# Expert units in one phase per batch behind the middle attention stage, both expert counts in one visit, three query buffers

## The chip, the cores and the metric

The kernel runs on one core of one Trainium2 chip. The metric is the device time of an execution in microseconds, the median of three: 462.71 us (462.43 to 462.92). Engines are called as in the profile: PE is TensorE (PEld its weight loads), DVE VectorE, ACT ScalarE, POOL GpSimd, SP the engine that issues most DMAs. Lines such as L251 are lines of the kernel before.

## The reference

Multi-query attention feeds a mixture of experts. Attention has 8 batches, 16 query heads of 384 positions by 64 features, and one key and value head per batch:

```
scores = (q @ k.T) / 8;  attn = softmax(scores);  o = attn @ v
x = o, rearranged to 3072 tokens x 1024 features
```

Each token goes to one of 4 groups and one of the group's 4 experts (16 in all), by two argmaxes:

```
g_idx = argmax(x @ w_group);  e_idx = argmax(x @ w_expert[g_idx])
y = relu(x @ w1[g_idx, e_idx]) @ w2[g_idx, e_idx]
out = softmax weight of the group * softmax weight of the expert * y
```

The weights w1 and w2 are 1024 x 1024 per expert. Inputs are float32.

## The kernel before, in words

**Stages.** The sequence of a batch is cut into three tiles of 128 query positions. One tile is a *stage* p, 0 to 23; p = 3b + st, b the batch, st the tile. A stage computes on PE scores of tile p (`scores`, L251: six key blocks j of 64 keys, 8 matmul records each), and the value products of tile p-1 (`values`, L290, also six blocks). ACT takes the exponential of each score block into a tile `pt` (L253). DVE adds the six blocks of a tile up (`pre_add`, L259 and L261), folds the sum over keys (`fold_keys`, L265), and PE sums the folded tile over partitions (`join`, L273: it reads `fold`). DVE inverts and spreads the sums (`invert`, L278 and L280) and multiplies the values by them (`weigh`, L300), which gives x of the tile, transposed; POOL casts it to bf16. The value products accumulate in a single buffer `o`, so values of tile p start only when tile p-1 is weighed. The join of tile p-1 stands in the middle of stage p, after its third value block.

**Turning the queries.** The queries come in with positions on partitions in blocks; DVE turns them (`prep_q`, L243) into a tile `qT` with two buffers, `prep_k` (L233) turns the keys.

**Experts.** Attention over nearly equal weights makes the tokens of a batch alike, so almost all of them go to one expert: for each batch one expert is chosen on the chip, its weights are loaded, and all 384 tokens of the batch go through it, with a gate of zero where a token belongs elsewhere. The work for a batch is a list of fourteen *units*: eight first-layer units (`h_unit`, L407: 8 matmuls of 384 columns, ACT applies relu, L408) and six second-layer units (`y_unit`, L415: 8 matmuls of 512 columns, ACT scales by the selected gate `gsel`, L416, and the row tile `y` is stored). `fill(n)` (L451 on) runs the next n units of whatever batch is next.

**Choice and counts.** `gates(b)` runs the gate matmuls (L312) on PE and the argmax and softmax arithmetic on DVE: for the first tile of batch b (`choose_a`) and for the other two of batch b-1 (`gate_math`; its one-hot is L373). `counts(now, full)` (L333 on) counts expert use by a matmul with ones: for the first tile of batch `now` (L338), from which `choose_b` picks the expert and POOL issues its weight loads (L145, L357), and for all of batch `full` (L340), from which `gate_c` marks pairs of batch and expert still missing and makes `gsel`. ACT copies the counts out of PSUM (L342).

**The leftover pair.** One pair of batch and expert that isn't covered is known early (`early_pair`, L508 on); its weights are loaded by `leftover_w1` and `leftover_w2` when a fixed number of units has run, and its few tokens are gathered, computed and scattered at the end. If more were missing, a slow path behind a branch would take over. `bound_a` and `bound_b` (L478 on) test a bound on the scores for which a softmax without its maximum is safe.

**What sets the order.** The order of instructions on every engine is the order in which this program calls the functions; each engine works through its own in that order, with semaphores between them. `PHASES` (L497) says how many units follow a stage: a *phase* stands between the end of a stage and the next stage's scores. In a phase, `steps` names what is called after which unit. Batch 0's first three units stand inside stage 4. After stage 23 the last join, values and weigh follow, and the last twenty units are spread among the work on the leftover pair.

Of the kernel before, what the change touches and what calls it, by code (L numbers as in the profile page):

```python
# [9 lines left out]
FP32 = mybir.dt.float32  # L10
# [3 lines left out]
P = 128  # L14
# [7 lines left out]
def kernel(  # L22
# [96 lines left out]
    def load_first():  # L119
        kt = pool.tile([P, ST, 2, D], FP32, tag="k", bufs=2, name="kn")  # L120
        qt = pool.tile([P, ST, HP, 2, D], FP32, tag="qraw", bufs=2, name="qn")
        for a in range(2):
            nc.scalar.dma_start(out=kt[:, :, a], in_=kn)
        for c in range(2):
            hs = slice(c * HC, (c + 1) * HC)
            for a in range(2):
                (nc.scalar if c and a else nc.sync).dma_start(out=qt[:, 0, hs, a], in_=qn[0, :, a, hs])
        for a in range(2):
            nc.sync.dma_start(out=qt[:, 1, :, a], in_=qn[1, :, a])
        k_raw[0], q_raw[0] = kt, qt  # L130
        load_k(1)
        load_v(0)
        for a in range(2):
            nc.sync.dma_start(out=qt[:, 2, :, a], in_=qn[2, :, a])
        qe_in = q[1].rearrange("(a hp) (st p) d -> st p a hp d", a=2, p=P)
        qe = pool.tile([P, HP, 2, D], FP32, tag="y", bufs=4, name="qe")
        for a in range(2):
            nc.sync.dma_start(out=qe[:, :, a], in_=qe_in[0, :, a])
        q_nat.append(qe)
# [80 lines left out]
        nc.vector.tensor_copy(out=kT[0][:], in_=ps[:, 0:S])  # L220

    def turn_q(p, nat, copies):
        qT[p] = pool.tile([P, 2 * CW], FP32, tag="qT", bufs=2, name="qT")
        n = HP // len(copies)
        for i, copy in enumerate(copies):
            ps = side([P, 2 * CW], FP32, "qps")
            for h in range(n):
                nc.tensor.transpose(out=ps[:, h * P:(h + 1) * P], in_=nat(i * n + h).rearrange("p a d -> p (a d)"), identity=ident[:])
            copy(out=qT[p][:, i * n * P:(i + 1) * n * P], in_=ps[:, 0:n * P])  # L229
# [9 lines left out]
        return q_raw[b][:, :, st * (P // 32):(st + 1) * (P // 32)].rearrange("p h k d -> p h (k d)")  # L239

    def prep_q(p):
        qT[p] = pool.tile([P, 2 * CW], FP32, tag="qT", bufs=2, name="qT")
        nc.vector.transpose(out=qT[p][:].rearrange("p (h n) -> p h n", h=HP), in_=q_of(p))  # L243

    def scores(p, j):
# [87 lines left out]
    def counts(now, full):  # L333
        n = GE * (1 + ST)
        ps = side([P, n], FP32, "cps")
        lo, hi = (0 if now is not None else GE), (n if full is not None else GE)
        if now is not None:
            nc.tensor.matmul(out=ps[:, 0:GE], lhsT=ones_bf[:], rhs=first[now][:].rearrange("p g e -> p (g e)"), start=True, stop=True)  # L338
        if full is not None:
            nc.tensor.matmul(out=ps[:, GE:n], lhsT=ones_bf[:], rhs=ohe_t[full][:].rearrange("p s g e -> p (s g e)"), start=True, stop=True)  # L340
        t = pool.tile([P, n], FP32, tag="cnt1", bufs=2, name="cnt1")
        nc.scalar.copy(out=t[:, lo:hi], in_=ps[:, lo:hi])  # L342
        if now is not None:
            seen[now] = t[:, 0:GE]
            choose_b(now, t[:, 0:GE])
        if full is not None:
            gate_c(full, t[:, GE:n])
# [78 lines left out]
    def first_units(b):  # L426
        rows = {}

        def place(st, cs):
            if cs.start == 0:  # L430
                rows[st] = pool.tile([P, Dm], FP32, tag="y", bufs=4, name="y")
            return rows[st][:, cs]

        def store(st, cs, y):
            if cs.stop == Dm:
                nc.sync.dma_start(out=outv[b, :, st, :], in_=rows[st][:])
        return moe_units(wts[b][0], wts[b][1], xbf[b], lambda: gsel[b], place, store)
# [13 lines left out]
    def fill(n):  # L451
        while n > 0:
            if not units:
                if begun[0] >= B or begun[0] not in wts:
                    return
                units.extend(first_units(begun[0]))
                begun[0] += 1
            units.pop(0)()
            n -= 1
            ran[0] += 1  # L460
            if ran[0] == (FO + 2 * ST) * (B - 2) + FO:
                leftover_w1()
            if ran[0] == (FO + 2 * ST) * (B - 1):
                leftover_w2()

    def gates(b):
        if b == 0:
            choose_a(0, gate_a(0, 0, 1))
            return
        ps = gate_a(b, 0, ST)  # L470
        choose_a(b, ps)
        gate_logits(b - 1, ps, 1, ST)
        gate_math(b - 1)
# [4 lines left out]
    def bound_a():  # L478
        sq = pool.tile([P, 2], FP32, tag="sq", bufs=1, name="sq")
        nc.vector.reduce_max(out=sq[:, 0:1], in_=stat_q[:], axis=AX)  # L480
        nc.vector.reduce_max(out=sq[:, 1:2], in_=stat_k[:], axis=AX)
        bound["sq"] = sq
# [11 lines left out]
        nc.vector.tensor_copy(out=oki[:], in_=okf[:])  # L494
        bound["okf"] = okf

    PHASES = {4: 5, 6: 7, 7: 6, 9: 7, 10: 6, 12: 7, 13: 6, 15: 7, 16: 6, 18: 7, 19: 6, 21: 7, 22: 7, 23: 5}  # L497

    def gates_and_turns(p):
        b = p // ST  # L500
        gates(b)
        if b + 1 < B:
            prep_k(b + 1)
            prep_q(p + 2)

    leftover = {}

# [38 lines left out]
    for p in range(NP):  # L546
        b, st = divmod(p, ST)
        jobs = [lambda: gates(0), lambda: None, lambda: counts(0, None)] if p == 2 else []
        if p == 0 or p == ST or (st == 1 and 1 < b < B - 1):
            load_q(b + 1)  # L550
        for j in range(3):
            scores(p, j)
            if p == 0 and j == 0:
                turn_q(1, lambda h: q_raw[0][:, 1, h], [nc.vector.tensor_copy])
        if p == 0:
            stats_k(0)
            prep_k(1)
        elif p == ST:
            prep_q(p + 1)
        if jobs:  # L560
            jobs.pop(0)()
        for j in (1, 2):
            pre_add(p, j)
        for j in range(KB):
            if p > 0:
                values(p - 1, j)
            if j == 2 and p > 0:
                join(p - 1)
            if j + 3 < KB:
                scores(p, j + 3)  # L570
            if 0 < j < 4:
                pre_add(p, j + 2)
            if j == 2 and p > 0:
                invert(p - 1)
            if j == 3:
                stats_q(p)
                if p == 1:
                    turn_q(2, lambda h: q_raw[0][:, 2, h], [nc.scalar.copy])
                elif p == 2:
                    turn_q(3, lambda h: q_nat[0][:, h], [nc.scalar.copy])  # L580
            if jobs:
                jobs.pop(0)()
            if p == ST + 1 and j == 0:
                fill(3)
            if st == 1 and 0 < b < B - 1 and j == 0:
                load_k(b + 1)
            if 0 < j < 5:
                some_q(1 if p <= ST + 1 else 2)
            if st == 1 and b + 1 < B and j == KB - 1:
                load_v(b + 1)  # L590
        assert not jobs
        if p > 0:
            weigh(p - 1)
        fold_keys(p)
        if st == 2 and b + 1 < B:
            stats_k(b + 1)
        if p in PHASES:
            n = PHASES[p]
            steps = {}
            if st < 2:  # L600
                prep_q(p + 1)
            if st == 0:
                counts(None, b - 2)
            elif st == 1:
                steps = {2: lambda: gates_and_turns(p), n - 1: lambda: counts(b, None)}
            else:
                bound_a()
                steps = {0: lambda: (counts(None, b - 1), early_pair()), n - 1: bound_b}
            for i in range(n):
                fill(1)  # L610
                if i in steps:
                    steps[i]()
# [6 lines left out]
    fill(2)  # L619
    gate_logits(last, gate_a(last, 1, ST), 1, ST)  # L620
    gate_math(last)
    fill(2)
    counts(None, last)

    xe = pool.tile([P, KO, S], BF16, tag="qraw", bufs=2, name="xe")
    nc.sync.dma_start(out=xe[:].rearrange("p k s -> p (k s)"), in_=xb_dram[bass.ds(leftover["b"], 1)].rearrange("a p k -> (a p) k"))
# [63 lines left out]
    for ko in range(KO):  # L690
        for st in range(ST):
            nc.tensor.matmul(out=px[:, ko, :], lhsT=xtok[st][:, ko * P:(ko + 1) * P], rhs=pick_bf[:, st, :], start=(st == 0), stop=(st == ST - 1))
    xc = pool.tile([P, KO, CAP], BF16, tag="qT", bufs=2, name="xc")
    nc.vector.tensor_copy(out=xc[:], in_=px[:])

    w1c, w2c = leftover["w1"], leftover["w2"]
# [6 lines left out]
    phT = side([P, 2, P], BF16, "phT")  # L703
    for h in range(2):
        nc.tensor.transpose(out=phT[:, h, :], in_=hg[:, h * P:(h + 1) * P], identity=ident_bf[:])
    hc = pool.tile([P, 2, P], BF16, tag="qT", bufs=2, name="hc")
    nc.vector.tensor_copy(out=hc[:], in_=phT[:])
    py = side([P, QW], FP32, "py")
    for g in range(4):
# [153 lines left out]
```

## Time and profile before

| what | value |
|---|---|
| time | 462.71 us (462.43 to 462.92) |
| span of the profiled execution | 462.0 us, granted PE clock 0.994 |
| PE busy | 450.8 us |
| DVE busy | 305.7 us |
| ACT busy | 242.6 us |
| POOL busy | 60.4 us |
| score matmuls (L251) and value matmuls (L290) | 142.8 and 141.0 us |
| unit matmuls, first layer (L407) and second (L415) | 87.4 and 85.4 us |
| loads of expert weights from issue to landing | 10.1 us (quarter of w1), 21.6 us (w2) |

Engines work side by side, so their busy times don't add up to the span. Matmuls are pipelined and their ends are modelled: the durations printed for neighbouring matmuls overlap, and the distance between the starts of two pieces is the better measure of what a piece costs.

### The profile page before, as it was taken

How to read it: one execution, taken by the hardware profiler on the slowest of the kernel's cores; microseconds unless marked ns; L12 is line 12 of the kernel's file. 1: busy time of each engine (PE TensorE's matmuls, PEld its weight loads, DVE VectorE, ACT ScalarE, POOL GpSimd, SP SyncE). 2: the span in 40 equal slices, each digit the busy share in tenths (PEclk: the TensorE clock that was granted, in tenths of full speed). 3: DMA queues.
4: the chain of work that ended last, by engine and by line, in shares of the span. 5: the costliest groups of instructions: out<-in, count | busy, mean ns of one | idle time of the engine just before them, and what ended most of it. 6: DMA issues, size and time to landing. Idle time of an engine off the chain costs nothing. (4 is left out here: it accounts for less than half of the span.)

```text
span 462.0 us, 10131 instructions
## 1 busy us (share of the span) xinstructions
PE 450.8 (98%) x4191; PEld 199.3 (43%) x4191; DVE 305.7 (66%) x483; ACT 242.6 (53%) x351; POOL 60.4 (13%) x83
## 2 busy tenths in 40 slices
PE   8999999999999999999999999999999999999992
PEld 6333444333533445343533435343443535344641
DVE  3999967964879286973779475992779564764400
ACT  2967645636366454745366364745457363623331
POOL 1004003000031002100030001300030000330000
PEclk9999999999999999999999999999999999999997
DMA  7697996998479691996759684996749712799981
GB/s 150 94 153 106 216 215 103 198 252 181 78 116 210 212 191 29 195 226 157 153 88 210 182 163 101 174 234 140 163 90 207 171 47 91 121 212 260 286 218 61
DMA packets 152165, 74.56 MB, mean 161 GB/s; under 512 B 120216, under 2 KB 138652, under 8 KB 152112
## 3 DMA queue, kind: packets, MB, share of 16 engines
q0 software_dynamic: 28416, 37.84, 47.2%
q1 hardware_dynamic: 122368, 35.68, 32.5%
q8 instruction: 35, 0.57, 0.5%
q10 hardware_dynamic: 1328, 0.33, 0.4%
q14 instruction: 18, 0.15, 0.1%
HBM read 92.62 MB, written 19.01 MB: 242 GB/s over the span
## 5 line engine op out<-in xcount | busy, mean ns | idle before, releaser
L253 ACT ACTIVATE pt<-s 128x1024 f32<-128x1024 f32 x144 | 142.1, 1026 | 67.2 <-PE s L251 66.4
L251 PE MATMUL s<-qT,kT 64*64 64x512 f32 x1152 | 142.8, 595 | 0.2 <-ACT qT L229 0.2
L290 PE MATMUL o<-pt,v 64*64 64x512 f32 x1152 | 141.0, 590 | 0.0
L261 DVE TENSOR_TENSOR presum<-presum,pt 128x1024 f32<-128x1024 f32 x96 | 116.6, 1215 | 16.3 <-ACT pt L253 10.9
L407 PE MATMUL hps<-xbf,w 128*128 128x384 bf16 x512 | 87.4, 326 | 0.0
L415 PE MATMUL yps<-w,hT 128*128 128x512 bf16 x384 | 85.4, 379 | 0.6 <-ACT y L416 0.6
L290 PEld LDWEIGHTS o<-pt,v 64*64 64x64 f32 x1152 | 43.5, 133 | 76.9 <-issue 73.2
L259 DVE TENSOR_TENSOR presum<-pt 128x1024 f32<-128x1024 f32 x24 | 29.4, 1224 | 69.3 <-ACT pt L253 68.5
L251 PEld LDWEIGHTS s<-qT,kT 64*64 64x64 f32 x1152 | 40.2, 133 | 64.3 <-issue 52.2
L416 ACT ACTIVATE y<-yps,gsel 128x512 f32<-128x512 f32 x48 | 32.6, 686 | 61.9 <-PE yps L415 49.9
L407 PEld LDWEIGHTS <-w 128*128 128x128 bf16 x512 | 48.6, 98 | 35.7 <-issue 4.1
L301 POOL CAST xbf<-xT 128x1024 bf16<-128x1024 f32 x24 | 25.0, 1041 | 280.8 <-DVE xT L300 280.8
L408 ACT ACTIVATE hT<-hps 128x384 bf16<-128x384 f32 x64 | 31.3, 488 | 51.0 <-PE hps L407 44.0
L415 PEld LDWEIGHTS <-hT 128*128 128x128 bf16 x384 | 36.8, 98 | 47.7 <-issue 4.9
L145 POOL DMA_DIRECT2D w<-in_moe_w_dram x36 | 24.8, 708 | 77.8 <-issue 58.7
L300 DVE TENSOR_TENSOR xT<-o,rinv 128x1024 f32<-128x1024 f32 x24 | 29.2, 1215 | 3.7 <-PE o L290 3.7
L280 DVE STREAM_TRANSPOSE rinv<-rc 128x1024 f32<-128x1024 f32 x24 | 29.9, 1245 | 0.8
L265 DVE TRANSPOSE_TENSOR_REDUCE fold<-presum 128x32 f32<-128x1024 f32 x24 | 29.6, 1232 | 0.0
L243 DVE STREAM_TRANSPOSE qT<-qraw 128x1024 f32<-128x1024 f32 x20 | 24.1, 1202 | 0.0
L209 ACT ACTIVATE qraw<-qraw 128x1024 f32<-128x1024 f32 x21 | 22.0, 1049 | 0.0
L318 DVE STREAM_TRANSPOSE L<-gps 128x32 f32<-128x32 f32 (+1 forms) x16 | 3.6, 227 | 17.4 <-PE gps L312 17.4
L273 PEld LDWEIGHTS sm<-fold,sel 64*64 64x64 f32 x192 | 7.2, 133 | 12.9 <-issue 12.9
(143 smaller groups left out, 158.2 us busy)
## 6 DMA issues: line engine op xcount, KB each, us to landing
w<-in_moe_w_dram POOLq DMA_DIRECT2D x36, 512.0 KB, 10.1
w<-in_moe_w_dram POOLq DMA_DIRECT2D x9, 2048.0 KB, 21.6
out_dram<-y SPq DMA_DIRECT2D x24, 512.0 KB, 2.8
qraw<-in_q_dram SPq DMA_DIRECT2D x56, 192.0 KB, 3.8
x_bf<-xbf SPq DMA_DIRECT2D x8, 768.0 KB, 4.6
v<-in_v_dram SPq DMA_DIRECT2D x16, 96.0 KB, 2.9
k<-in_k_dram SPq DMA_DIRECT2D x28, 48.0 KB, 2.6
qn<-in_q_dram SPq DMA_DIRECT2D x4, 256.0 KB, 5.0
```

The source lines that it names most:

```text
L251: nc.tensor.matmul(out=ps[64 * c:64 * c + 64, a, :], lhsT=kT[b][r, j * D:(j + 1) * D], rhs=qT[p][r, c * CW:(c + 1) * CW], start=True, stop ...
L253: nc.scalar.activation(out=t[:], in_=ps[:], func=ACTF.Exp, scale=scale)
L259: nc.vector.tensor_add(out=presum[p][:], in0=pt[p, 0][:], in1=pt[p, 1][:])
L261: nc.vector.tensor_add(out=presum[p][:], in0=presum[p][:], in1=pt[p, j][:])
L265: nc.vector.tensor_reduce(out=fold[p][:], in_=presum[p][:].rearrange("p a (n i) -> p (a n) i", i=32), axis=AX, op=OP.add, apply_transpose= ...
L280: nc.vector.transpose(out=t[:].rearrange("p (b i) -> p b i", i=32), in_=rc[:].rearrange("p c b -> p (c b)").unsqueeze(2).to_broadcast([P, ...
L290: nc.tensor.matmul(out=o_ps[p][64 * a:64 * a + 64, c, :], lhsT=v_sb[b][r, j, :], rhs=pt[p, j][r, a, :], start=(j == 0), stop=(j == KB - 1))
L300: nc.vector.tensor_mul(out=xT[b][:, :, ts], in0=o_ps[p][:].rearrange("p c (h n) -> p (c h) n", n=P), in1=rinv[p][:].rearrange("p (h n) -> ...
L407: nc.tensor.matmul(out=ps[:, 0:S], lhsT=w1[:, ko, fc * P:(fc + 1) * P], rhs=xb[:, ko, :], start=(ko == 0), stop=(ko == KO - 1))
L408: nc.scalar.activation(out=state["h"][:, fc, :], in_=ps[:, 0:S], func=ACTF.Relu)
L415: nc.tensor.matmul(out=ps[:], lhsT=state["h"][:, fo, st * P:(st + 1) * P], rhs=w2[:, fo, nh * CW:(nh + 1) * CW], start=(fo == 0), stop=(fo ...
L416: nc.scalar.activation(out=y, in_=ps[:], func=ACTF.Copy, scale=gs_of()[:, st:st + 1])
```

## The change

Before, units follow two stages of each batch: stage 3b (st = 0) and stage 3b+1 (st = 1), 14 phases of five to seven units. The full count of batch b-2 stands at the head of the first phase and the choice for batch b at the end of the second. After, all fourteen units of a batch follow its middle stage, st = 1, in one phase; there are seven phases, behind stages 4, 7, 10, 13, 16, 19 and 22. The first has eleven units (three still stand in stage 4), the last has eight, and none follow stage 23; the number of units before the last join is 92 as before. In a phase, the gates come after its third unit, and after its fifth one visit that counts for the choice of batch b and for the full count of batch b-1. Then the keys and two query tiles of the next batch are turned; with the turn at the head of the phase, all three turns of a batch lie in it, for which qT gets a third buffer and y gives one up. The early pair is worked out in the phase behind stage 22, and the bound on the scores goes behind the last stage's gates.

```diff
-        qe = pool.tile([P, HP, 2, D], FP32, tag="y", bufs=4, name="qe")
+        qe = pool.tile([P, HP, 2, D], FP32, tag="y", bufs=3, name="qe")
...
-        qT[p] = pool.tile([P, 2 * CW], FP32, tag="qT", bufs=2, name="qT")
+        qT[p] = pool.tile([P, 2 * CW], FP32, tag="qT", bufs=3, name="qT")
...
-    PHASES = {4: 5, 6: 7, 7: 6, 9: 7, 10: 6, 12: 7, 13: 6, 15: 7, 16: 6, 18: 7, 19: 6, 21: 7, 22: 7, 23: 5}
-
-    def gates_and_turns(p):
+    UNITS = FO + 2 * ST
+    PHASES = {ST * b + 1: UNITS for b in range(1, B - 1)}
+    PHASES[ST + 1] -= 3
+    PHASES[NP - 2] = FO
+
+    def turns(p):
         b = p // ST
-        gates(b)
         if b + 1 < B:
             prep_k(b + 1)
             prep_q(p + 2)
+            prep_q(p + 3)
...
             n = PHASES[p]
             steps = {}
-            if st < 2:
-                prep_q(p + 1)
-            if st == 0:
-                counts(None, b - 2)
-            elif st == 1:
-                steps = {2: lambda: gates_and_turns(p), n - 1: lambda: counts(b, None)}
-            else:
-                bound_a()
-                steps = {0: lambda: (counts(None, b - 1), early_pair()), n - 1: bound_b}
+            prep_q(p + 1)
+            steps = {2: lambda: gates(b), 4: lambda: (counts(b, b - 1), turns(p))}
+            if b == B - 1:
+                steps[5] = early_pair
             for i in range(n):
                 fill(1)
                 if i in steps:
                     steps[i]()
...
     gate_math(last)
+    bound_a()
     fill(2)
     counts(None, last)
+    bound_b()
```

More of the change, by code (lines that the diff above doesn't have):

```diff
@@ L241, in prep_q @@
     def prep_q(p):
-        qT[p] = pool.tile([P, 2 * CW], FP32, tag="qT", bufs=2, name="qT")
+        qT[p] = pool.tile([P, 2 * CW], FP32, tag="qT", bufs=3, name="qT")
         nc.vector.transpose(out=qT[p][:].rearrange("p (h n) -> p h n", h=HP), in_=q_of(p))
@@ L430, in place @@
             if cs.start == 0:
-                rows[st] = pool.tile([P, Dm], FP32, tag="y", bufs=4, name="y")
+                rows[st] = pool.tile([P, Dm], FP32, tag="y", bufs=3, name="y")
             return rows[st][:, cs]
@@ L692 @@
             nc.tensor.matmul(out=px[:, ko, :], lhsT=xtok[st][:, ko * P:(ko + 1) * P], rhs=pick_bf[:, st, :], start=(st == 0), stop=(st == ST - 1))
-    xc = pool.tile([P, KO, CAP], BF16, tag="qT", bufs=2, name="xc")
+    xc = pool.tile([P, KO, CAP], BF16, tag="qT", bufs=3, name="xc")
     nc.vector.tensor_copy(out=xc[:], in_=px[:])
@@ L705 @@
         nc.tensor.transpose(out=phT[:, h, :], in_=hg[:, h * P:(h + 1) * P], identity=ident_bf[:])
-    hc = pool.tile([P, 2, P], BF16, tag="qT", bufs=2, name="hc")
+    hc = pool.tile([P, 2, P], BF16, tag="qT", bufs=3, name="hc")
     nc.vector.tensor_copy(out=hc[:], in_=phT[:])
```

## The prediction

> **What bounds the kernel now.** First the page, for the busy shares:
>
> ```profile
> PE 450.8 (98%) x4191; PEld 199.3 (43%) x4191; DVE 305.7 (66%) x483; ACT 242.6 (53%) x351; POOL 60.4 (13%) x83
> ```
>
> TensorE (PE) looks full, but the ends of matmuls are modelled, so 98% is no proof. Stronger is the timeline of PE alone, read by its *starts*: the distance from one start to the next is what a piece costs. Stages 5 and 6, with the phase behind stage 6 (columns: start, duration, instruction, count, idle before):
>
> ```profile
> 83.87 2.75 PE L251 MATMUL s<-qT,kT 64*64 64x512 f32 x24
> 86.44 1.04 PE L290 MATMUL o<-pt,v 64*64 64x512 f32 x8
> ...
> 91.71 2.75 PE L290 MATMUL o<-pt,v 64*64 64x512 f32 x24
> 94.40 0.20 PE L340 MATMUL cps<-ohe,ones_bf 128*128 128x48 bf16 x1
> 94.44 5.34 PE L415 MATMUL yps<-w,hT 128*128 128x512 bf16 x24
> 100.36 5.34 PE L415 MATMUL yps<-w,hT 128*128 128x512 bf16 x24 [0.58 <-ACT y L416]
> 105.53 1.46 PE L407 MATMUL hps<-xbf,w 128*128 128x384 bf16 x8
> 106.93 2.81 PE L251 MATMUL s<-qT,kT 64*64 64x512 f32 x24
> ```
>
> There is one hole, 0.58 us. From such starts I take unit costs: a bare attention stage 10.42 us (the scores of stage 5 start at 73.40 + 10.47, of which 0.05 is paid for coming out of a phase); a first-layer unit 1.303 (three in 3.91); a second-layer unit 1.726 (six in 10.36 near the end); the gate 1.46. **PE's own order is the bound**; only what PE pays between pieces, and holes, can move the time.
>
> Then the last stage, 23, on PE, and under it on VectorE (DVE):
>
> ```profile
> 400.39 2.75 PE L290 MATMUL o<-pt,v 64*64 64x512 f32 x24
> 403.08 1.47 PE L407 MATMUL hps<-xbf,w 128*128 128x384 bf16 x8
> ...
> 409.62 0.38 PE L487 MATMUL pq<-ident,sq 128*1 128x128 f32 x2
> 409.93 0.30 PE L273 MATMUL sm<-fold,sel 64*64 64x16 f32 x8
> 410.07 5.36 PE L290 MATMUL o<-pt,v 64*64 64x512 f32 x48
> ```
>
> ```profile
> 402.62 1.18 DVE L261 TENSOR_TENSOR presum<-presum,pt 128x1024 f32<-128x1024 f32 x1
> 403.72 1.22 DVE L300 TENSOR_TENSOR xT<-o,rinv 128x1024 f32<-128x1024 f32 x1
> 404.86 1.23 DVE L265 TRANSPOSE_TENSOR_REDUCE fold<-presum 128x32 f32<-128x1024 f32 x1
> ```
>
> DVE ends the fold of stage 23 (L265) at 406.09, about 3 us after the stage's last value matmul. PE doesn't notice: five expert units stand between, and the join (L273), which reads the fold, comes at 409.93.
>
> Last, two answers by stretch (length, busy us of PE, PEld, DVE, ACT, POOL, then granted clock, DMA share, GB/s): stage 5, and 1 us slices past the last matmul group, which starts at 453.70 and lasts 1.06:
>
> ```profile
> 83.87:94.40 10.53, 10.53 (x109) 3.64 (x101) 9.92 (x10) 7.26 (x10) 1.04 (x1) 1.00 1.19 209
> ```
>
> ```profile
> 456.00:457.00 1.00, 0.00 (x0) 0.00 (x0) 0.00 (x0) 0.00 (x0) 0.67 (x1) 0.95 0.09 25
> 457.00:458.00 1.00, 0.00 (x0) 0.00 (x0) 0.00 (x0) 0.00 (x0) 0.00 (x0) 0.50 0.28 86
> ```
>
> DVE is 94% busy in a bare stage, and the clock falls to half at 456.9 (a mean of 0.95 is 0.1 us of half clock).
>
> [...] No run here shows a matmul overtaking another. [...] the trace shows the fold starting only as the weighing before it ends (404.86 after 403.72 + 1.22).
>
> **The change part by part.**
>
> *Fewer phases.* Take from start-to-start distances the unit costs. Phase behind stage 9: its scores start at 137.45, those of stage 10 at 159.77, 22.32 in all, less 10.42, one first-layer unit 1.30 and six second-layer units 10.36, leaves 0.24. Stages 12, 15, 18 and 21 leave 0.23 each by the same sum. The next stage's first scores take 0.05 more than bare: 0.29 for such a visit, full count included. Phase behind stage 7: 106.93 to 126.98 is 20.05, less 10.42, six units 7.82 and the gate 1.46, leaves 0.35 (0.05 of it for coming out of the phase before). A batch pays 0.64. One phase of fourteen pays the way in (0.11 on the last values, 0.09 on the first unit), the way out (0.09 after second-layer units, 0.05 on the scores) and two count matmuls amid units at 0.03 each (404.39 to 404.42), 0.40 in all. Six batches (stages 6/7 to 21/22) save 6 x 0.24 = **-1.4 us**.
>
> *The hole at stage 6.* The six second-layer units there cost 11.09 (94.44 to 105.53) against 10.36. They wait for the selected gates, whose full count is queued behind weigh, fold and a query turn on DVE. In the new phase the count comes at step 4, when those are done; about 2.5 us of DVE work (the choice and six small operations) then has the first two second-layer units to hide behind, and two more score buffers are free. **-0.7 us.**
>
> *One count visit.* Seven ACT copies go (0.17 to 0.20 us each, L342) and ACT is 53% busy: nothing. A new wait: the counting matmul of the previous batch needs the one-hot made by the gate just before. In the phase of stage 4 the gate ends at 70.69 and that one-hot (L373) at 72.58; two units bring PE to 73.30. It fits by 0.7 us: nothing.
>
> *Query turns and buffers.* The same turns (1.20 us on DVE each), now three in one phase, hidden behind 20 us of units; one buffer of 4 KB a partition moves from y to qT, and y needs three rows per batch. Nothing. Three attention stages now run without a phase; DVE is 94% busy there, but waits 0.26 us for ACT within stage 5, so lag isn't carried over. Nothing, with up to 0.3 us a batch (2 us) as the upper bound.
>
> *Behind stage 23 no units are left.* This is the big term. The join now follows the last values directly. In the trace of before, scores of stage 23 start at 392.50, a stage out of a phase takes 10.47, so PE reaches the join at 402.97; the fold ends at 406.09, and DVE-to-PE release costs 0.07 (xc ends 451.42, the next matmul starts 451.49). PE waits **+3.2 us**, and the 48 value matmuls queue behind. Saved against it: the visit behind stage 23 took 22.86 (392.50 to 415.36), less 10.42, five units 6.52 and bare values 5.15, leaves 0.77; the new order keeps 0.05 in, 0.10 join, 0.11 out, so -0.5, of which 0.3 (pq) returns at the end, where PE sat 0.42 for the loaded x (L681) and hides it. DVE's bound work (0.84 us) moves ahead of the ranks, whose matmul had 0.5 us to spare and gains 0.3: +0.1. Net of this part **+2.7 to +2.8**.
>
> *Leftover weights* are asked for a stage earlier and nothing waited for them: nothing.
>
> Sum without the clock: 462.7 - 1.4 - 0.7 + 2.75 = **463.3**.
>
> *The clock.* [...] I take 1.5 with the halving as the likelier. **464.8.**
>
> **The rivals.**
> - *The hole, but full clock*: 463.3. [...]
> - *Three bare stages make DVE the bound*: 2 us more, 466.8. For it: 94%. Against: DVE's waits for ACT in stage 5.
> - *Faster*: the hole at the join is small because fold comes sooner, or is made good later, and the -2.1 stands: 461.0. For it: phases really cost what the starts say. Against: DVE's order puts weigh and fold behind the last values wherever a stage ends.
>
> **How the numbers follow.** Forecast 0.47, full clock 0.28, DVE bound 0.10, faster 0.15. Range: 462.3 (between the faster case and full clock, with 0.5 us of error on the phase costs) to 466.5 (just under the DVE case). Chances: slower is the forecast, the DVE case and a fifth of the full-clock case, 0.63; same is most of the full-clock case, 0.23; faster 0.14.
>
> **What would show it.** A wait of PE at L273 near 3.2 us ahead of the last values; right behind it, value matmuls with start distances doubled for up to 3.4 us and a granted clock of 0.5; no hole at L415 near 75 us; start distances of 0.4 us over the bare work per batch. It is wrong if PE's third bare stage takes over 10.5 us, if second-layer units wait in the first phase, or if the wait at L273 is under 2.5.

## The result and the profile after

The changed kernel took 465.25 us (median of six, 464.25 to 465.79) beside 462.94 us for the kernel before (six, 462.43 to 463.28): ratio 1.0050, 95% interval 1.0037 to 1.0063. Measured again later it took 464.53 us (fourteen, 463.33 to 466.90) beside 463.15: 1.0033, 1.0019 to 1.0047. It is slower, by between 0.2% and 0.6%. The forecast was 464.8, made from 462.71 us for the kernel before: 2.1 us more, where the two measurements give 2.3 and 1.4 more.

The busy shares of the changed kernel, from its page:

```profile
PE 449.6 (97%) x4182; PEld 199.9 (43%) x4191; DVE 306.3 (66%) x483; ACT 242.1 (52%) x344; POOL 60.4 (13%) x83
```

They say nothing of a loss. PE's share is a microsecond below that of before, but nine of its records are missing from this trace (4182 beside 4191), so the difference can't be trusted; ACT has its seven copies fewer. The timeline of PE tells it, first where the change was meant to gain (start, duration, instruction, count, idle before): the end of stage 4's phase, then the first scores of stages 5, 6 and 7, and those that follow the next phase.

```profile
70.31 2.77 PE L407 MATMUL hps<-xbf,w 128*128 128x384 bf16 x16
72.92 0.17 PE L338 MATMUL cps<-ohe,ones_bf 128*128 128x16 bf16 x1
72.95 0.18 PE L340 MATMUL cps<-ohe,ones_bf 128*128 128x48 bf16 x1
72.97 10.52 PE L415 MATMUL yps<-w,hT 128*128 128x512 bf16 x47
83.42 2.81 PE L251 MATMUL s<-qT,kT 64*64 64x512 f32 x24
...
93.89 2.75 PE L251 MATMUL s<-qT,kT 64*64 64x512 f32 x24
...
104.31 2.75 PE L251 MATMUL s<-qT,kT 64*64 64x512 f32 x24
...
114.83 4.07 PE L407 MATMUL hps<-xbf,w 128*128 128x384 bf16 x24
...
137.31 2.81 PE L251 MATMUL s<-qT,kT 64*64 64x512 f32 x24
```

The reader is to see: both counts cost 0.05 us amid the units; the six second-layer units run through, 10.45 us with the way out, where before they took 11.09 with a hole; the second bare stage in a row is 10.42 us (93.89 to 104.31), and the third 10.52 (104.31 to 114.83), of which the prediction's 0.11 is the way into the units, so a third stage costs no more; a period is 53.89 us (83.42 to 137.31), 0.39 over the bare work of 53.50 (three stages 31.26, eight units 10.42, six units 10.36, gate 1.46).

Then the last stage, 23, and what follows:

```profile
396.41 2.81 PE L251 MATMUL s<-qT,kT 64*64 64x512 f32 x24
...
404.30 2.75 PE L290 MATMUL o<-pt,v 64*64 64x512 f32 x24
410.14 0.30 PE L273 MATMUL sm<-fold,sel 64*64 64x16 f32 x8 [3.09 <-DVE fold L265]
410.25 7.08 PE L290 MATMUL o<-pt,v 64*64 64x512 f32 x48
417.27 3.63 PE L415 MATMUL yps<-w,hT 128*128 128x512 bf16 x15
...
425.35 0.38 PE L487 MATMUL pq<-ident,sq 128*1 128x128 f32 x2
426.26 3.61 PE L415 MATMUL yps<-w,hT 128*128 128x512 bf16 x16 [0.53 <-ACT y L416]
```

PE stands 3.09 us at the join, for the fold, and none of the 48 value matmuls queued behind it starts before 410.25. They take 7.02 us from start to start, where before they took 5.29. The answer by stretch, the one at half clock and one as long on either side (length, busy us of PE, PEld, DVE, ACT, POOL, then granted clock, DMA share, GB/s), shows why:

```profile
406.92:410.33 3.41, 0.32 (x16) 0.22 (x16) 3.08 (x3) 0.00 (x0) 1.04 (x1) 1.00 1.16 210
410.33:413.74 3.41, 3.41 (x28) 1.26 (x27) 1.60 (x2) 0.00 (x0) 0.00 (x0) 0.50 1.13 214
413.74:417.16 3.42, 3.42 (x36) 1.23 (x28) 0.00 (x0) 0.00 (x0) 0.00 (x0) 1.00 1.12 211
```

The clock is at half for 3.41 us, from 410.33 to 413.74, and full on either side; the 3.41 us ahead hold 0.32 us of matmuls. Such a stretch at half clock is the window of the expectations below. In it the value matmuls, which come in groups of four, stand 0.85 us apart from group to group (411.08 to 413.64), behind it 0.43 (414.12 to 416.70). DVE, for whose fold PE waits, is busy through the stretch ahead:

```profile
406.53 1.18 DVE L261 TENSOR_TENSOR presum<-presum,pt 128x1024 f32<-128x1024 f32 x1
407.63 1.22 DVE L300 TENSOR_TENSOR xT<-o,rinv 128x1024 f32<-128x1024 f32 x1
408.76 1.23 DVE L265 TRANSPOSE_TENSOR_REDUCE fold<-presum 128x32 f32<-128x1024 f32 x1
```

**Where the time went**, from starts on PE in the two profiled executions:

| stretch | before | after | difference |
|---|---|---|---|
| start to the scores of stage 4 | 50.53 | 50.15 | -0.38 |
| stage 4 to stage 23, less the five units (6.52) and one count (0.03) that moved in | 341.97 | 346.26 - 6.55 | -2.26 |
| stage 23 and last values, before less the same units and the count | 22.86 - 6.55 | 20.86 | +4.55 |
| from there to the last matmul group | 38.34 | 38.66 | +0.32 |

The sum is 2.23 us, which is the distance of the last matmul groups (453.70 and 455.93); the spans differ by 2.0. The first line isn't of the change: it arises ahead of the first stages (their long run of scores starts at 10.64 and at 10.25 us) and stays the same up to stage 4. The trace's record of full clock begins at 6.34 us in one execution and at 4.14 in the other: up to there the warm-up matmuls (L152, L442) start 0.107 us apart, and in the changed kernel, which has some left then, 0.056 us apart behind it.

### The profile page after: what moved, and what is told of

Its sections match the earlier page's. It is cut to its first block, busy times and chain, and to the rows that moved or that the text cites. A ratio compares the mean times of both kernels' runs of the same rounds, so it can differ in the third digit from the quotient of the medians.

```text
span 464.0 us, 10148 instructions
## 1 busy us (share of the span) xinstructions
PE 449.6 (97%) x4182; PEld 199.9 (43%) x4191; DVE 306.3 (66%) x483; ACT 242.1 (52%) x344; POOL 60.4 (13%) x83
## 5 line engine op out<-in xcount | busy, mean ns | idle before, releaser
L290 PE MATMUL o<-pt,v 64*64 64x512 f32 x1152 | 142.7, 596 | 0.0
L415 PE MATMUL yps<-w,hT 128*128 128x512 bf16 x375 | 84.0, 379 | 1.0 <-ACT y L416 0.5
```

What stands on the lines that cost most here:

```text
L290: nc.tensor.matmul(out=o_ps[p][64 * a:64 * a + 64, c, :], lhsT=v_sb[b][r, j, :], rhs=pt[p, j][r, a, :], start=(j == 0), stop=(j == KB - 1))
L415: nc.tensor.matmul(out=ps[:], lhsT=state["h"][:, fo, st * P:(st + 1) * P], rhs=w2[:, fo, nh * CW:(nh + 1) * CW], start=(fo == 0), stop=(fo ...
```

## The experiments

**Two units ahead of the join.** The hole is filled with work that is there anyway.

```diff
+    fill(2)
     join(NP - 1)
     for j in range(KB):
         values(NP - 1, j)
```

> The changed kernel with two of the tail's second-layer units (3.45 us of TensorE work) moved ahead of the join behind stage 23; the tail has two fewer. Theory (hole at the join costs 3.1 us, and halves the clock for one window, 1.7 us more): the wait of PE at L273 goes to zero, the granted clock stays 1.00 until the last matmul, and a switch into and out of the units costs about 0.3 us: 465.25 - 3.1 - 1.6 + 0.3 = 460.9 us, below the kernel before. Rival (the phases themselves are slower and the hole is hidden work shifted about): about 465. Second rival (clock is not affected by the hole): 462.5.

Measured: 461.85 us (twelve) beside 463.04, ratio 0.9973 (0.9964 to 0.9981); a second time 461.93 beside 463.13, 0.9971 (0.9963 to 0.9979). Its timeline of PE:

```profile
407.60 3.63 PE L415 MATMUL yps<-w,hT 128*128 128x512 bf16 x15
411.15 0.31 PE L273 MATMUL sm<-fold,sel 64*64 64x16 f32 x8
411.29 5.36 PE L290 MATMUL o<-pt,v 64*64 64x512 f32 x48
...
424.64 0.19 PE L340 MATMUL cps<-ohe,ones_bf 128*128 128x48 bf16 x1
424.67 0.38 PE L487 MATMUL pq<-ident,sq 128*1 128x128 f32 x2
425.67 2.76 PE L407 MATMUL hps<-xbf,w 128*128 128x384 bf16 x16 [0.63 <-ACT cnt L342]
428.54 0.18 PE L643 MATMUL pr<-mb,prefix 128*128 128x4 bf16 x1
```

No wait at the join, and the values at 5.29 us. The clock is full until the last matmul, by the answer for that stretch:

```profile
6.60:453.50 446.90, 443.82 (x4134) 195.01 (x4142) 304.43 (x469) 239.99 (x341) 57.70 (x69) 1.00 0.84 164
```

With this one line the change is faster than the kernel before, so the merged phases do gain, and the hole is what lost it. It missed the expected 460.9 by 0.95: two waits of 0.6 us each appear in the tail, the first ahead of the units at 425.67, the other ahead of and between the ranks' matmuls (L643). For the first the view names ACT's copy of the counts, which frees a score buffer; there are three of these, and the bound's transposes (`pq`) hold one until DVE reads it:

```profile
426.98 0.40 DVE L489 TENSOR_REDUCE bd<-pq 1x2 f32<-1x256 f32 x1
```

**Spare matmuls in the hole.** The join starts when it did, but PE is busy for most of the wait.

```diff
+    spare = side([P, CW], FP32, "spare")
+    for _ in range(40):
+        nc.tensor.matmul(out=spare[:, 0:P], lhsT=ones_bf[:], rhs=ones_bf[:], start=True, stop=True)
     join(NP - 1)
```

> The changed kernel with 40 spare bf16 matmuls of 128 columns (about 2.2 us, results unused) ahead of the join behind stage 23, so the join still waits for the fold until the same moment but PE is busy in most of the hole. Theory with the clock: the join starts when it did, the clock stays full, the 48 value matmuls behind it take 5.3 us and not 7.0: 465.25 - 1.6 = 463.6 us. Theory without the clock (the values are slow for another reason, such as their inputs): 465.2 us, values still 7.0 us.

Measured: 464.33 us (seven, 463.01 to 464.81) beside 463.04, 1.0026 (1.0013 to 1.0039). Its timeline of PE:

```profile
406.88 2.41 PE L613 MATMUL spare<-ones_bf 128*128 128x128 bf16 x40
410.04 0.30 PE L273 MATMUL sm<-fold,sel 64*64 64x16 f32 x8 [0.75 <-DVE fold L265]
410.15 5.39 PE L290 MATMUL o<-pt,v 64*64 64x512 f32 x48
415.47 3.63 PE L415 MATMUL yps<-w,hT 128*128 128x512 bf16 x15
```

The join starts at 410.04, 13.73 us after the stage's scores (396.31), as in the changed kernel (410.14 after 396.41), and the same values take 5.32 us and not 7.02. The granted clock is full over join and values:

```profile
410.04:415.47 5.43, 5.43 (x56) 2.15 (x57) 1.60 (x2) 0.00 (x0) 0.00 (x0) 1.00 1.12 213
```

So the clock, not their inputs, made them slow: 1.7 us within an execution. The median fell by less, 0.2 to 0.9 us against the two measurements of the changed kernel, because the clock doesn't fall in all its executions. Of its twenty, eight lie at 463.3 to 464.3 and twelve at 464.8 to 466.9; the medians of the two groups, 464.0 and 465.6, are 1.6 us apart. The mean granted clock recorded with each execution parts them in the same way: 0.993 to 0.997 in the eight, 0.988 to 0.992 in the twelve, and 0.993 to 0.997 in all seven with the spare matmuls. For a single execution this is a sign and no proof, since those of the kernel before, which have no such hole, range from 0.991 to 0.997.

**The kernel before, with only the last phase moved.** The five units behind stage 23, with their count, the early pair and the bound, follow the last weighing.

```diff
-        if p in PHASES:
+        if p in PHASES and p < NP - 1:
...
     weigh(NP - 1)
+    bound_a()
+    for i in range(PHASES[NP - 1]):
+        fill(1)
+        if i == 0:
+            counts(None, B - 2)
+            early_pair()
+    bound_b()
```

> The kernel before with one change: the five units behind stage 23, with their counts and the early pair, follow the last weighing and no longer stand ahead of the last join. All other phases as before. Theory: the same hole appears here alone, PE waits 3.1 us at L273 and the values behind it lose 1.6 us to the clock, less 0.2 us for a phase switch: 462.9 + 4.5 = 467.4 us, and 465.8 in an execution whose clock holds. Rival (the loss of the change lies in the merged phases, not at the join): 462.9 us.

Measured: 468.26 us (five, 466.58 to 468.85) beside 463.04, 1.0104 (1.0086 to 1.0122). Its timeline of PE:

```profile
406.54 0.41 PE L273 MATMUL sm<-fold,sel 64*64 64x16 f32 x8 [3.08 <-DVE fold L265]
406.74 6.91 PE L290 MATMUL o<-pt,v 64*64 64x512 f32 x48
413.58 1.47 PE L407 MATMUL hps<-xbf,w 128*128 128x384 bf16 x8
...
438.58 0.62 PE L685 MATMUL pb<-ident_bf,xe 128*128 128x128 bf16 x8 [0.72 <-DMA xe<-x_bf]
```

Hole and half clock (6.84 us of values) appear with all other phases as before: this part of the change alone makes the loss. Within these values the clock is at half:

```profile
408.00:410.00 2.00, 2.00 (x12) 0.56 (x8) 0.64 (x1) 0.00 (x0) 0.00 (x0) 0.53 1.14 215
```

The loss is 5.2 us and not 4.5; part of the rest is the wait for the loaded x, 0.72 us in this execution and 0.42 in that of the kernel before.

**The kernel before, with the full count ahead of the query turn.**

```diff
-            if st < 2:
-                prep_q(p + 1)
             if st == 0:
                 counts(None, b - 2)
-            elif st == 1:
+            if st < 2:
+                prep_q(p + 1)
+            if st == 1:
```

> The kernel before with one change: in the phases behind a batch's first stage the full count is called ahead of the query turn, so DVE makes the selected gates 1.2 us sooner. Theory: the hole of 0.58 us at the second-layer units behind stage 6 closes and nothing else moves: 462.9 - 0.6 = 462.3 us. Rival (the hole comes from the score buffers or the store of y, not from DVE's order): 462.9 us with the hole still there.

Measured: 462.27 us (22) beside 463.04, 0.9985 (0.9978 to 0.9992). Its timeline of PE behind stage 6:

```profile
93.98 0.20 PE L340 MATMUL cps<-ohe,ones_bf 128*128 128x48 bf16 x1
94.02 10.52 PE L415 MATMUL yps<-w,hT 128*128 128x512 bf16 x47
104.38 1.46 PE L407 MATMUL hps<-xbf,w 128*128 128x384 bf16 x8
```

The six units take 10.36 us without a hole. The hole of before was DVE's order. It is worth 0.77 us between medians (0.4 to 1.0 by the interval), and the prediction gave it 0.7.

**A shorter hole.** As with the 40 spare matmuls, but 18. Two outcomes: the clock stays full in every execution, or it still falls in part of them.

> The changed kernel with 18 spare bf16 matmuls of 128 columns (about 1.0 us) ahead of the join, so that the hole at L273 is about 2.1 us and not 3.1; the join starts when it did. [...] it stays full in every execution: 463.7 to 464.3 us, as with 40 spare matmuls. [...] median about 465.

Measured: 464.36 us (seven, four at 464.0 to 464.4 and three at 465.2 to 465.8) beside 463.15, 1.0033 (1.002 to 1.0046). In the profiled execution (465.35) the hole is 1.98 us and the values take 7.02 again; by stretch:

```profile
407.54:410.95 3.41, 1.44 (x29) 1.07 (x29) 2.90 (x4) 0.00 (x0) 1.04 (x1) 1.00 1.16 212
410.95:414.37 3.42, 3.42 (x20) 1.29 (x16) 1.42 (x2) 0.00 (x0) 0.00 (x0) 0.50 1.12 213
```

The clock doesn't stay full in every execution: here it is at half (0.50) behind 3.41 us with 1.44 us of matmuls, 42%. Three of the seven executions lie in the upper group, with a granted clock of 0.991 where the other four have 0.993 or 0.994. The median is the slowest of the lower group and says little.

**The changed kernel again.**

> The changed kernel once more, beside the others on the same chip. Theory: PE waits 3.1 us at L273 in each execution, and the clock is halved for one window in most: 465.2 us, with single executions near 463.9 where it is not.

Measured: 464.53 us, given above; 0.7 lower than expected, with seven of fourteen executions at 463.3 to 464.3. The profiled one (464.79, mean granted clock 0.992) shows the wait of 3.09 us and 7.02 us of values.

**The bound on the scores worked out earlier**, on top of the two units ahead of the join.

```diff
     invert(NP - 1)
+    bound_a()
     weigh(NP - 1)
+    bound_b()
...
     gate_math(last)
-    bound_a()
     fill(2)
     counts(None, last)
-    bound_b()
```

> As the kernel with two units ahead of the join, and the bound on the scores is worked out during the last values: its two maxima behind the inversion, its transposes and small DVE operations behind the last weighing, where DVE is idle. Theory (in the previous kernel PE stood 0.6 us ahead of the first-layer units for a score buffer that the bound's transposes held, and 0.6 us ahead of the ranks for DVE, both because the bound's DVE work sat in the queue there): both waits go, 461.85 - 1.2 = 460.7 us. Rival (these waits have another cause, the chain from the counts alone): 461.8 us.

Measured: 461.91 us (eleven) beside 463.15, 0.9975 (0.9966 to 0.9985): no gain over the two units alone. Its timeline of PE:

```profile
424.21 2.76 PE L407 MATMUL hps<-xbf,w 128*128 128x384 bf16 x16
427.17 0.18 PE L643 MATMUL pr<-mb,prefix 128*128 128x4 bf16 x1 [0.20 <-DVE mb L635]
...
434.22 0.62 PE L682 MATMUL pb<-ident_bf,xe 128*128 128x128 bf16 x8 [0.76 <-DMA xe<-x_bf]
```

The wait for the score buffer is gone, so the bound's transposes were its cause. The ranks come sooner too, 2.99 us behind the count (L340, at 424.18) and not 3.90, but PE waits for them no less: they start 2.96 us behind the units ahead of them, and 2.87 us before, as these units start sooner as well. Then PE stands 0.76 us for the loaded x. That this wait ate the gain isn't shown, for the second profiled execution of the two units alone, without the early bound, has the same one:

```profile
435.05 0.62 PE L682 MATMUL pb<-ident_bf,xe 128*128 128x128 bf16 x8 [0.77 <-DMA xe<-x_bf]
```

Its first had none. Over the eleven profiled executions of this document the load took 6.7 to 8.6 us from issue to landing, so a single execution of each kernel doesn't tell why the gain is missing.

**The load of x issued behind the last weighing**, on top of that. The two lines go from their later place.

```diff
     weigh(NP - 1)
+    xe = pool.tile([P, KO, S], BF16, tag="qraw", bufs=2, name="xe")
+    nc.sync.dma_start(out=xe[:]..., in_=xb_dram[bass.ds(leftover["b"], 1)]...)
     bound_b()
```

> As the kernel with units ahead of the join and the early bound, and the load of x for the leftover pair is issued right behind the last weighing, ahead of the two stores of y in SP's queue. Theory (the early bound's gain went into a new wait of PE for that load at L682, 0.76 us): the wait goes and the gain shows, 461.9 - 0.8 = 461.1 us. Rival (something else at the end sets the time): 461.9 us.

Measured: 461.21 us (five, 460.12 to 461.33) beside 463.13, 0.9955 (0.9941 to 0.9969), beside 461.93 for the two units alone on the same chip. In the profiled execution, the fastest of the five, PE doesn't wait at L682:

```profile
430.64 2.76 PE L407 MATMUL hps<-xbf,w 128*128 128x384 bf16 x16
433.27 0.62 PE L682 MATMUL pb<-ident_bf,xe 128*128 128x128 bf16 x8
```

The median is the lowest of all, though its interval overlaps a little with that of the two units alone. The reason isn't the one given: the load was issued at 426.5 us in this execution and at 426.3 in the one before, since SP stood 7.5 us ahead of it for the store of x (`x_bf`) that it reads. It landed after 6.7 us and not 7.8, and the two stores of y now follow it in SP's queue. Whether that shortened the landing, or whether it is the spread seen above, stays open.

## Why the prediction was right

- *The number*: 464.8 is the forecast for an execution whose clock falls behind the hole, by the author's estimate the likelier case; it fell in five of the first six executions and in seven of the later fourteen, by the two groups above. That the first median came as near as 0.45 us owes something to that draw; the later one is 0.27 below. The rival with a full clock, 463.3, describes the eight other executions (463.3 to 464.3).
- *Unit costs from starts*: a period is 0.39 us over its bare work; forecast 0.40. Stage 4 to stage 23 gained 2.26 us; forecast 1.4 for fewer phases and 0.7 for the hole at stage 6. The count-first experiment shows the 0.7 apart from the rest (0.77 between medians).
- *Counts in one visit, turns, buffers, three bare stages, leftover weights at nothing*: right. The one-hot (L373) ended at 72.21 and PE reached the count at 72.92, the 0.7 us to spare that the prediction read; the third bare stage takes 10.52 us, 10.41 without the way into the units, like the second. The rival with DVE as the bound falls.
- *The hole at the join*: 3.09 us; forecast 3.2. The changed order of the last phase alone makes it (third experiment), filling it takes it away (first). One reading behind it was a little off: the prediction's fold starts at 404.86, 0.08 us before the weighing ends (403.72 + 1.22 is 404.94). The two keep their order, but overlap that much.
- *The clock*: the step that carried the forecast past 463.3. Half clock for 3.41 us behind the hole costs 1.76 us on the values (7.02 against 5.26, the prediction's 5.15 and 0.11); forecast 1.5, the author's estimate, with the halving as the likelier case. The spare matmuls show that it is the clock. In the kernel before the clock falls to half only behind the last matmuls, at 456.90, and the 3.41 us ahead of that hold 1.06 us of matmuls (31%); behind the hole it fell with 1.44 us (42%) ahead of it too.
- *The tail*, the term that was off: forecast +0.1 beyond what is hidden, measured +0.32. The prediction let the bound's DVE work delay the ranks; what it delayed first was the release of the score buffer that the transposes (L487) hold until DVE reads it at 427.36, so that a second-layer unit stood 0.53 us for another one. The early bound, tried on the kernel with two units ahead, takes such a wait away. The wait for x, 0.42 before, is gone in both profiled executions of the changed kernel, as foreseen.
- *The rival "faster"*: DVE's order did put weigh and fold behind the last values. It came true only once the hole was filled, at 461.9 and 461.2 us.

## What to carry to other kernels

When work is merged into fewer, larger blocks, look at the places that lose their block: there a wait that had always been covered comes into the open, here 3 us at the one join that no longer had units ahead of it. Gains of a saturated engine can be counted from start to start, small as they are, but one hole of 3.1 us cost more than all of them here (2.3 us), and in twelve of twenty executions, by their times, it cost the clock besides. Filling it with two units of later work kept the merge's gain: 461.9 us, beside 463.0 without the merge.

## What the runs showed of the hardware that was not expected

- The 3.41 us ahead of a half clock were not always near empty: behind the hole it came after 1.44 us of matmuls (42%) in the kernel with 18 spare ones. At the ends of the kernels, where the matmuls are small, by the modelled times half clock came after 1.73 us (51%) in the kernel with 40 spare matmuls, and full clock after 1.96 us (57%) in the first run of the two units ahead. The two lines of each:

```profile
452.59:456.00 3.41, 1.73 (x50) 0.98 (x38) 0.29 (x1) 0.86 (x2) 0.00 (x0) 1.00 0.32 132
456.00:459.41 3.41, 0.00 (x0) 0.00 (x0) 0.00 (x0) 0.00 (x0) 1.09 (x1) 0.50 0.12 37
```

```profile
450.67:454.09 3.42, 1.96 (x58) 1.21 (x50) 0.29 (x1) 0.86 (x2) 0.00 (x0) 1.00 0.42 161
454.09:457.50 3.41, 0.00 (x0) 0.00 (x0) 0.00 (x0) 0.00 (x0) 1.09 (x1) 1.00 0.13 40
```

- How short the hole must be for the clock to stay full isn't shown. With 3.09 us of it twelve of twenty executions show a loss, by their times; with 1.98 us three of seven.
- The 40 spare matmuls, which leave a hole of 0.75 us, kept the clock full behind it in the profiled execution and, as far as the recorded clocks tell, in the six others.
- The clock stays full from 4.14 to 410.33 us in the changed kernel and from 6.34 to 456.90 in the kernel before. Behind the hole it doesn't fall in every execution, so the same hole costs 3.1 us in some and 4.8 in others; what decides between them isn't shown. The 4.8 was seen in both profiled executions of the changed kernel; that others lose only the hole is read from their times and clocks, as no profile caught one.
